# A decayed linear attention with a Fourier mix and an MLP: five instruction queues written anew

## The chip, the cores and the metric

The kernel runs on one core of one Trainium2 chip. The metric is the device time of one execution in microseconds (us). A core has five engines with a queue each: TensorE (PE, matmuls), ScalarE (ACT), VectorE (DVE), GpSimd (POOL) and SyncE (SP, which here only issues transfers). A queue is worked off in its written order, and an instruction that waits for a semaphore holds up all that stand behind it on the same engine.

## The reference

There are 4 batches, 8 heads, 768 positions and a head width of 48, so 384 model columns. The reference, cut to what matters:

```python
for t in range(S):                                   # per batch and head
    y[t]  = r[t] @ (state + outer(u * k[t], v[t]))
    state = w[t][:, None] * state + outer(k[t], v[t])
x = y.transpose(0, 2, 1, 3).reshape(B, S, 384)
u = x + real(fft(fft(x, axis=1), axis=2))            # Fourier mix
un = (u - mean(u)) / sqrt(var(u) + 1e-6)
out = u + maximum(un @ w_ch1, 0) @ w_ch2             # 384 -> 1536 -> 384
```

## The kernel before

**Work.** A batch is cut into 6 chunks of 128 positions. For each chunk the *attention* part takes the logarithm of w (line 754), sums it by a matmul with a triangular mask (756, 760, 766/769), takes exponentials (762, 775), multiplies r and k by them (794, 797), transposes both (810 and 816 on TensorE, for the last batch 802 by a transfer), forms the 128 x 128 products of all heads (826), masks them (839), updates the state (860, 868) and sums the output (881/884, added to v times the bonus in 890). Batch 0 does this for two chunks at a time, with its own lines (607 to 736; the product of k and decay is line 659, its transposes 666, the masks 688, the state 704/708, the outputs 722 to 730). The bonus is r times k (642 or 779), times u (643 or 781), a sum over the head (644 or 783) and the product with v (647 or 786). Line 789 casts v.

The *mix* part of a batch folds the attention's output by symmetry (901 to 922), multiplies by cosine and sine tables (948), copies and mirrors the result (953, 957), multiplies again (971), adds x (973), takes mean and variance (977, 979), writes the normalized rows (983), transposes them (994/997, or for batches 2 and 3 a transfer, line 1000), and then for each half of a batch runs the MLP: 12 x 3 matmuls of 384 columns (1018), the ReLU (1025 on ScalarE, 1023 on VectorE), 3 x 12 matmuls (1036), the last sum (1040) and the output (1044). Batches overlap: the mix of batch b runs beside the attention of batch b+1.

**Order.** Each operation is made once, in program order, with a number, its reads and its writes; from these `place` and `emit` derive the semaphores. The order on each queue does not follow from the program: `ORDER` holds, for each of the five queues, the list of operation numbers in the order of issue, and so also says which engine does an operation that may run on several (`vec`: POOL or VectorE; `evict`: ScalarE or VectorE). `BANKS` holds, for each of the 8 PSUM banks, the order in which tiles use it; a tile waits for the former tile of its bank.

```python
def place(self, order, banks):
    self.order = {e: [self.ops[int(i)] for i in order[e].split()] for e in self.ENGS}
    for e in self.ENGS:
        for o in self.order[e]:
            o.eng = e
            o.fn = o.alts[e][1]
```

**Loads.** All loads of w, k, r and v are issued by SyncE (494 for batch 0, 384 KB each; 500 for the others, 192 KB each), into 7 buffers per tensor, so a load also waits until its buffer's former content has been read. The two weight matrices (1152 KB each, line 587) are issued by POOL. The outputs (1044) and the transposing transfers (802, 1000) stand in SyncE's queue among the loads.

**Filler matmuls.** Eight matmuls at the start (1056) and `NW` more (1073), which read a constant tile and whose results nobody reads, are placed by `ORDER` like any other.

**Numbers used below.** On the start (batch 0): 43, 93, 140 are the loads of w for chunks 0/1, 2/3, 4/5; 48, 95, 142 those of k; 47, 94, 141 those of r. 50, 97, 144 are the logarithms; 54, 57 the exponentials of the first pair of chunks, 101, 104 those of the second. 66, 68 are the products of k and decay of chunks 0 and 1; 113, 115 of chunks 2 and 3 (the second pair, "chunk 2" in the lists). 60, 61, 62 are the first pair's bonus steps. In batch 1, 368 is the load of k of chunk 0 and 376 its product with r. In batch 3, 1175 is r times k of chunk 4; 1124 the product of k and decay of chunk 2.

Of the kernel before, what the change touches and what calls it, by code (L numbers as in the profile page):

```python
# [22 lines left out]
NW = 12  # L23
# [10 lines left out]

W_AFTER = {"W1": (0, 4, "w"), "W2": (1, 0, "r")}
# [26 lines left out]
    "act": (  # L62
# [12 lines left out]
    "dve": (  # L75
# [14 lines left out]
    "pool": (  # L90
# [12 lines left out]
}  # L103

BANKS = (
# [220 lines left out]
def bass_rwkv6_finch__then__fnet_fourier_mix_kernel(  # L326
# [19 lines left out]
    NJ = HID // 128  # L346
# [760 lines left out]
```

## Time and profile before

| | |
|---|---|
| median of 3 runs | 189.91 us (186.45 to 191.11) |
| the profiled execution's own time | 187.31 us |
| its span, first to last instruction | 185.5 us |
| mean granted TensorE clock | 0.991 |
| TensorE, VectorE, ScalarE, POOL busy | 95%, 84%, 64%, 54% |
| instructions on these | 1827 matmuls, 346, 280, 115 |
| bytes moved by transfers | 29.59 MB, mean 160 GB/s |
| instruction packets (two queues) | 0.23 MB and 0.06 MB |

A row of the table by stages gives the stretch in us, its length, then busy time and number of instructions for PE, weight loads, VectorE, ScalarE and POOL, the granted clock, the share of the 16 transfer engines and GB/s. Rows of groups give line, engine, operation, what is written and read, shapes, the count, busy us in all, mean ns of one, and the idle time before them with what ended it. Rows of the chain of work that ended last give start, length, and what it was. Rows of waits give us in all, times, and the longest. The mean length that stands for a matmul is that from its start to its modelled end; those of 384 columns have 326 ns there, and where nothing stops them 21 of them take 3.41 us.

### The profile page before, as it was taken

The numbers are of one execution on the slowest core, as the hardware profiler recorded it, in microseconds if no ns is written. First come the engines' busy times: TensorE is split into PE (matmuls) and PEld (weight loads), VectorE is DVE, ScalarE is ACT, GpSimd is POOL, SyncE is SP. The second block draws the span as 40 slices with busy tenths as digits, with TensorE's granted clock in tenths as the row PEclk, the third lists the DMA queues.
The fourth block names the chain that finished last, engine by engine and source line by source line (L and its number), as shares of the span: only waits on it lengthen the run. The fifth ranks groups of instructions, "written<-read, shape, count | busy, mean of one in ns | idle before, by whom it ended". The sixth has DMA issues, their size and how long they took to land.

```text
span 185.5 us, 4700 instructions
## 1 busy us (share of the span) xinstructions
PE 176.3 (95%) x1827; PEld 115.0 (62%) x1827; DVE 155.8 (84%) x346; ACT 119.3 (64%) x280; POOL 100.0 (54%) x115
## 2 busy tenths in 40 slices
PE   6986999998997999999999999998999999999994
PEld 2463776865565677666767765564676656565663
DVE  7599898799999989999999999998997938627034
ACT  3696699599989959789999585993452334222200
POOL 4186687599298744998997279959801000000000
PEclk9998799999999999999999999999999999999999
DMA  5999899899999999959677989988502131501233
GB/s 155 323 325 334 187 173 208 158 199 201 208 154 179 212 182 208 196 117 217 130 170 164 199 191 222 179 146 153 121 2 91 39 64 25 166 4 42 85 121 134
DMA packets 104151, 29.59 MB, mean 160 GB/s; under 512 B 98881, under 2 KB 103618, under 8 KB 104130
## 3 DMA queue, kind: packets, MB, share of 16 engines
q1 hardware_dynamic: 102178, 26.95, 65.3%
q0 software_dynamic: 1952, 2.36, 7.9%
q8 instruction: 14, 0.23, 0.4%
q14 instruction: 7, 0.06, 0.1%
HBM read 24.19 MB, written 4.72 MB: 156 GB/s over the span
## 4 chain that ended last, share of the span: by engine, by line
PE 70%; DVE 18%; DMA 6%; ACT 3%; issue 1%; SPq 0%; ACTq 0%
PE bank L1036 22%; PE bank L1018 19%; PE bank L971 5%; PE bank L948 5%; DVE ah L839 3%; DVE bst L977 2%; DMA unt<-un 2%; DMA in_v<-in_v_dram 2%; PE bank L826 2%; DMA in_w<-in_w_dram 2%; DVE uf L973 2%; PE bank L726 1%; PE bank L722 1%; DVE rkh L794 1%; PE bank L760 1%
## 5 line engine op out<-in xcount | busy, mean ns | idle before, releaser
L1018 PE MATMUL bank<-unt,w 128*128 128x384 bf16 x288 | 55.5, 326 | 0.6 <-DMA unt<-un 0.5
L1036 PE MATMUL bank<-w,ht 128*128 128x384 bf16 (+2 forms) x300 | 53.3, 320 | 0.0
L1025 ACT ACTIVATE ht<-bank 128x384 bf16<-128x384 f32 x74 | 34.4, 496 | 28.3 <-PE bank L1018 28.1
L1036 PEld LDWEIGHTS bank<-w,ht 128*128 128x128 bf16 x300 | 27.8, 98 | 15.9
L1018 PEld LDWEIGHTS bank<-unt,w 128*128 128x128 bf16 x288 | 26.3, 97 | 16.2 <-DMA unt<-un 0.9
L451 POOL TENSOR_TENSOR rkh<-in_k,e 128x384 bf16<-128x384 f32 x20 | 20.6, 1028 | 9.9 <-ACT e L634 8.4
L1040 DVE SCALAR_TENSOR_TENSOR osb<-bank,rstd,uf 128x384 f32<-128x384 f32 (+2 forms) x25 | 14.8, 595 | 12.0 <-PE bank L1036 11.9
L839 DVE TENSOR_TENSOR ah<-bank,msk 128x512 bf16<-128x512 f32 x36 | 23.4, 676 | 0.4 <-PE bank L826 0.3
L474 ACT ACTIVATE rkt<-bank 128x512 bf16<-128x512 bf16 (+1 forms) x26 | 18.0, 712 | 5.0 <-PE bank L810 2.8
L451 POOL TENSOR_TENSOR rk<-rk,ub 128x384 f32<-128x384 f32 x17 | 16.9, 998 | 4.4 <-DVE rk L451 4.1
L451 POOL TENSOR_TENSOR rk<-in_r,in_k 128x384 f32<-128x384 f32 x16 | 16.2, 1022 | 2.9 <-DMA in_k<-in_k_dram 2.8
L451 POOL TENSOR_TENSOR vtd<-in_v,dc 128x384 f32<-128x384 f32 x17 | 14.3, 842 | 4.1 <-DVE dc L783 4.1
L1023 DVE TENSOR_SCALAR ht<-bank 128x384 bf16<-128x384 f32 x22 | 11.6, 547 | 5.5 <-PE bank L1036 5.1
L465 ACT ACTIVATE lb<-in_w 128x384 bf16<-128x384 f32 (+1 forms) x21 | 11.9, 571 | 2.5 <-DMA in_w<-in_w_dram 2.5
L973 DVE TENSOR_TENSOR uf<-bank,x 128x384 f32<-128x384 f32 x24 | 12.5, 545 | 0.6 <-PE bank L971 0.6
L977 DVE BATCH_NORM_STATS2 bst<-uf 128x6 f32<-128x384 f32 x24 | 12.9, 546 | 0.0
L948 PE MATMUL bank<-k,xf 128*128 128x193 bf16 (+1 forms) x84 | 11.6, 258 | 0.0
L890 DVE TENSOR_TENSOR x<-bank,vtd 128x384 f32<-128x384 f32 x18 | 9.9, 548 | 1.8 <-POOL vtd L451 1.1
L465 ACT ACTIVATE un<-uf,agg 128x384 bf16<-128x384 f32 x17 | 10.4, 627 | 0.1
L465 ACT ACTIVATE vb<-in_v 128x384 bf16<-128x384 f32 (+1 forms) x17 | 9.4, 558 | 1.6 <-DMA in_v<-in_v_dram 1.6
L794 DVE TENSOR_TENSOR rkh<-bank,in_r 128x384 bf16<-128x384 f32 x18 | 9.7, 546 | 0.4 <-ACT bank L762 0.4
L762 ACT ACTIVATE bank<-bank 128x384 f32<-128x384 f32 x18 | 8.7, 487 | 2.0 <-PE bank L756 2.0
(144 smaller groups left out, 355.9 us busy)
## 6 DMA issues: line engine op xcount, KB each, us to landing
out_dram<-osb SPq DMA_DIRECT2D x23, 192.0 KB, 2.0
in_w<-in_w_dram SPq DMA_DIRECT2D x18, 192.0 KB, 4.5
in_v<-in_v_dram SPq DMA_DIRECT2D x18, 192.0 KB, 4.0
in_r<-in_r_dram SPq DMA_DIRECT2D x18, 192.0 KB, 4.4
in_k<-in_k_dram SPq DMA_DIRECT2D x18, 192.0 KB, 4.3
w<-in_moe_w_ch_dram POOLq DMA_DIRECT2D x2, 1152.0 KB, 10.8
in_w<-in_w_dram SPq DMA_DIRECT2D x3, 384.0 KB, 4.7
in_k<-in_k_dram SPq DMA_DIRECT2D x3, 384.0 KB, 4.6
```

Source lines behind the costliest of these rows:

```text
L451: return lambda e: e.tensor_tensor(out=o, in0=a, in1=b, op=f)
L465: return lambda e: e.activation(o, a, f, **kw)
L474: {"act": lambda e: e.activation(o(), i(), ACTF.Copy), "dve": lambda e: e.tensor_copy(out=o(), in_=i())}, **kw)
L839: masked[n] = op("dve", v_1(512), lambda e, x=x: e.tensor_tensor(out=ah[:, x:H:2, :], in0=ps(ta[x])[:, :].rearrange("p (h t) -> p h t", t= ...
L948: return e.matmul(ps(t)[:, cols], x, tab[:, s % NP, cols], start=a, stop=z, skip_group_check=True)
L973: op("dve", v_1(DM), lambda e, kb=kb, t=t: e.tensor_tensor(out=uf[:, kb, :], in0=ps(t)[:, 0:DM], in1=xb[:, kb, 0:DM], op=ALU.add), r=[t, ( ...
L977: op("dve", v_1(DM), lambda e, kb=kb, bs=bs: e.bn_stats(bs[:, :], uf[:, kb, :]), r=[("UF", i, kb)], w=[("BST", n % 4)])
L1018: ins = e.matmul(ps(t)[:, 0:384], W1[:, m, 128 * j:128 * j + 128], unt[:, :, m, :], start=(m == 0), stop=(m == NM - 1))
L1023: {"dve": lambda e, j=j, t=t, ht=ht: e.tensor_scalar(out=ht[:, j, :], in0=ps(t)[:, 0:384], scalar1=-1.0, scalar2=0.0, op0=ALU.mult, op1=AL ...
L1025: "act": lambda e, j=j, t=t, ht=ht: e.activation(ht[:, j, :], ps(t)[:, 0:384], ACTF.Relu, scale=-1.0)},
L1036: ins = e.matmul(ps(t)[:, 0:hi - lo], ht[:, j, 128 * x:128 * x + 128], W2[:, j, lo:hi], start=(j == 0), stop=(j == NJ - 1))
L1040: op("dve", v_1(hi - lo) + 64, lambda e, kb=kb, t=t, o=o, lo=lo, hi=hi: e.scalar_tensor_tensor(out=o[:, lo:hi], in0=ps(t)[:, 0:hi - lo], s ...
```

## The change

`NW` goes from 12 to 20, and `ORDER` and `BANKS` are new in full. `W2C = 0` is a new switch; with 0 the weight's load and its use are what they were.

```diff
-NW = 12
+NW = 20
+W2C = 0
...
     "pe": (
-        "24 1383 1384 52 53 51 55 56 1385 98 99 45 70 100 69 71 72 81 1386 102 1387 103 87 1388 75 78 149 146 117 "
-        "147 116 119 145 1389 118 128 89 122 83 192 195 125 1390 163 162 1391 165 164 372 134 401 374 189 403 130 "
+        "1383 1384 24 1385 55 52 53 51 99 56 98 1386 45 102 70 100 72 103 81 69 71 146 87 1387 147 1388 117 1389 "
+        "1390 1391 75 78 119 145 116 118 128 1392 1393 1394 122 125 89 83 1395 149 1396 195 192 401 1397 403 372 "
+        "1398 189 374 162 164 1399 1400 163 1401 165 130 134 168 171 136 208 200 209 201 174 371 400 176 180 202 "
...
     "act": (
-        "0 50 54 97 58 59 57 46 101 105 73 74 144 104 106 111 148 121 152 120 151 150 90 193 196 370 399 84 166 "
+        "0 50 97 54 58 57 59 46 105 101 144 106 73 104 74 111 121 120 148 151 399 152 90 84 187 150 370 193 186 "
...
     "dve": (
-        "36 30 10 1 7 5 35 33 11 29 12 17 21 39 26 4 13 37 16 15 27 18 22 31 9 6 8 19 20 23 66 188 60 65 67 64 61 "
-        "82 62 107 88 112 80 115 114 76 77 79 109 160 129 124 158 123 194 127 126 154 155 135 169 170 173 172 175 "
+        "11 33 5 1 7 9 6 13 12 10 39 28 36 17 38 15 16 35 32 34 14 21 18 8 23 20 19 22 66 60 68 64 65 4 67 82 62 "
+        "107 112 88 114 77 79 76 188 80 123 126 109 129 160 127 158 124 194 190 154 155 135 170 173 169 172 175 "
...
     "pool": (
-        "2 42 38 3 41 34 25 68 113 32 28 63 108 153 159 161 110 91 86 85 132 156 92 139 138 178 376 198 207 405 "
+        "29 31 30 26 2 25 3 27 61 113 115 63 108 153 159 110 161 86 91 92 85 156 132 139 405 198 207 229 411 469 "
...
+        "835 834 882 865 1098 1092 1093 1066 1067 1175 1124 1176 1095 1069 1118 1150 1144 1119 1181 1145 1121 "
...
     "sp": (
-        "43 48 93 47 44 49 95 94 140 96 142 141 185 395 366 143 424 453 398 487 369 367 368 455 396 397 425 426 "
+        "43 93 48 47 44 49 140 95 94 96 142 141 395 185 366 143 424 367 396 454 453 369 398 397 368 426 455 487 "
...
-            asked[n] = op("pool", d, lambda e, T=T, x=x: e.dma_start(T[:, :, :], x.rearrange("(q p) n -> p q n", p=128)),
+            asked[n] = op("pool", d, lambda e, T=T, x=x, n=n: e.dma_start(
+                T[:, :, :], x.rearrange("(p q) n -> p q n" if n == "W2" and W2C else "(q p) n -> p q n", p=128)),
...
-                        ins = e.matmul(ps(t)[:, 0:384], W1[:, m, 128 * j:128 * j + 128], unt[:, :, m, :],
+                        ins = e.matmul(ps(t)[:, 0:384], W1[:, m, j::NJ] if W2C else W1[:, m, 128 * j:128 * j + 128], unt[:, :, m, :],
```

78 operations are on another engine than before. By kind of work (the line that makes them), the number that goes each way:

| line, work | |
|---|---|
| 578, 581 fills | 6 VectorE to POOL, 4 POOL to VectorE |
| 643 bonus times u, batch 0 | 1 VectorE to POOL (op 61) |
| 659 k times decay, batch 0 | 115 VectorE to POOL, 68 POOL to VectorE |
| 779 r times k | 2 VectorE to POOL, 1 POOL to VectorE (op 376) |
| 786 bonus times v | 1 VectorE to POOL (batch 1, chunk 3) |
| 789 cast of v | 3 VectorE to ScalarE |
| 797 k times decay | 1 POOL to VectorE |
| 819, 820 copies of transposed r, k | 6 ScalarE to VectorE, 3 VectorE to ScalarE |
| 901 fold, batch 0 | 2 POOL to VectorE |
| 915 to 920 folds | 8 VectorE to POOL, 2 POOL to VectorE |
| 953 copies in the mix | 4 VectorE to ScalarE |
| 957 mirrors in the mix | 2 POOL to ScalarE, 1 ScalarE to POOL |
| 983 normalized rows | 6 VectorE to ScalarE |
| 997 copies of transposed rows | 1 ScalarE to VectorE |
| 1022 ReLU | 11 ScalarE to VectorE, 9 VectorE to ScalarE |
| 549, 567 tables | 1 VectorE to ScalarE, 1 ScalarE to VectorE |

After it VectorE has 331 instructions instead of 346, ScalarE 288 instead of 280, POOL's list 118 instead of 111, TensorE's list 545 instead of 537; SyncE's 121 are the same in another order.

134 rows, old and new, of tables (BANKS, ORDER) are left out of this document.

## The prediction

> **What bounds the kernel now.** I read the page first, then the busy time by stages, then the chain that ended last, then the waits.
>
> ```profile
> span 185.5 us, 4700 instructions
> PE 176.3 (95%) x1827; PEld 115.0 (62%) x1827; DVE 155.8 (84%) x346; ACT 119.3 (64%) x280; POOL 100.0 (54%) x115
> ...
> PE 70%; DVE 18%; DMA 6%; ACT 3%; issue 1%; SPq 0%; ACTq 0%
> ```
>
> TensorE carries the chain for 70% of the span and VectorE for 18%, but not at the same time. So the stages:
>
> ```profile
> core 0: us, PE busy (x) PEld busy (x) DVE busy (x) ACT busy (x) POOL busy (x), PEclk, DMA share, GB/s
> 0.00:13.70 13.70, 11.50 (x129) 6.45 (x129) 10.52 (x42) 8.77 (x14) 6.08 (x16) 1.00 0.97 267
> 13.70:17.10 3.40, 1.74 (x25) 1.30 (x25) 3.40 (x5) 1.83 (x4) 2.67 (x2) 1.00 1.12 360
> 17.10:20.50 3.40, 3.36 (x32) 1.98 (x30) 3.27 (x6) 2.81 (x4) 2.68 (x2) 0.50 0.78 165
> 20.50:38.00 17.50, 17.50 (x303) 13.05 (x301) 15.00 (x29) 13.27 (x31) 12.28 (x16) 1.00 0.97 191
> 38.00:59.10 21.10, 19.02 (x218) 12.36 (x216) 21.03 (x47) 19.69 (x47) 17.54 (x19) 1.00 1.05 189
> 59.10:129.00 69.90, 69.20 (x755) 46.25 (x752) 67.27 (x145) 56.63 (x140) 53.56 (x59) 1.00 0.90 179
> 129.00:185.50 56.50, 53.98 (x380) 33.64 (x378) 35.30 (x78) 16.28 (x43) 5.15 (x6) 1.00 0.26 76
> ```
>
> Four stretches can be seen. Until 20.5 us loads and a stall bind. TensorE is busy for 1.74 of 3.40 us, and in the next 3.4 us its granted clock is 0.50. From 38.0 to 59.1 VectorE is never idle (21.03 of 21.10) and TensorE has 2.1 us of holes. From 59.1 to 129.0 both are full. After 129.0 TensorE alone is full up to the last output.
>
> ```profile
> 0.73 3.42 DMA in_w<-in_w_dram
> ...
> 6.23 0.50 ACT e L634
> ...
> 14.72 2.08 DVE rkh L451
> 16.84 0.42 PE bank L666 x4
> ...
> 55.32 0.47 DVE bank L868
> ...
> 124.53 3.84 DMA unt<-un
> 128.41 1.64 PE bank L1018 x9
> ...
> 155.65 3.41 PE bank L1018 x21
> ...
> 171.90 11.09 PE bank L1036 x80
> 183.02 0.35 DVE osb L1040
> ```
>
> The chain begins with a load, then hangs on one VectorE product of 2.08 us (k times the decay, line 659, chunk 2 of batch 0) for which the transposes of line 666 wait. It runs through VectorE up to 55.8 us, and at the end through matmuls 0.16 us apart (3.41 us for 21). So the span is the matmul work plus what TensorE loses before 59.1 us and a little at 124.5. A gain has to come from these; the stretch after 129.0 can only grow.
>
> **The change part by part.** The operations are the same but for eight more filler matmuls. W2C = 0 leaves the weight lines as they are, and the end is unchanged: last product, last output. All five queues, the engine of 78 operations and the PSUM banks are new. I follow the new lists with the durations of the old rows:
>
> ```profile
> L451 POOL TENSOR_TENSOR rkh<-in_k,e 128x384 bf16<-128x384 f32 x20 | 20.6, 1028 | 9.9 <-ACT e L634 8.4 <-ACT e L775 0.8 <-DMA in_k<-in_k_dram 0.6
> L451 DVE TENSOR_TENSOR rkh<-in_k,e 128x384 bf16<-128x384 f32 x4 | 3.7, 931 | 1.6 <-ACT e L634 1.6
> L451 DVE TENSOR_TENSOR vtd<-in_v,dc 128x384 f32<-128x384 f32 x1 | 1.3, 1349 | 0.0
> L791 DVE CAST vb<-in_v 128x384 bf16<-128x384 f32 x3 | 2.4, 790 | 0.0
> L475 DVE COPY rkt<-bank 128x512 bf16<-128x512 bf16 x4 | 1.7, 413 | 0.0
> L890 DVE TENSOR_TENSOR x<-bank,vtd 128x384 f32<-128x384 f32 x18 | 9.9, 548 | 1.8 <-POOL vtd L451 1.1 <-PE bank L884 0.5
> L475 DVE COPY unt<-bank 128x384 bf16<-128x384 bf16 x1 | 0.3, 340 | 0.0
> L1073 PE MATMUL bank<-ht 128*128 128x384 bf16 x12 | 4.3, 380 | 0.0
> ```
>
> *Term 1, up to 38.0 us.* The 2.08 us product (op 115) goes to POOL, where it takes 1.03 (first row), and in exchange op 68 of chunk 0 comes to VectorE (0.93). The second product of the bonus (op 61) goes to POOL too. On POOL the order is then 61, 113, 115, and op 115 waits for its exponential (op 104), which ScalarE reaches earlier because the third w load (op 140) is now issued ahead of op 95. I put the end of op 115 at 14.2 us instead of 16.8: its exponential, which starts at 13.43 in the rows below and ends at 13.9, ends 0.8 earlier without the logarithm of w (0.84) just ahead of it, and then 1.03 for the product. Against this stands the order of the loads. Each of these 384 KB pieces takes 1.2 us at the rate of this stretch:
>
> ```profile
> GB/s 155 323 325 334 187 173 208 158 199 201 208 154 179 212 182 208 196 117 217 130 170 164 199 191 222 179 146 153 121 2 91 39 64 25 166 4 42 85 121 134
> 12.67 0.84 ACT L465 ACTIVATE lb<-in_w 128x768 bf16<-128x768 f32 x1 [0.20 <-DMA in_w<-in_w_dram]
> 13.43 0.48 ACT L634 ACTIVATE e<-bank 128x392 f32<-128x392 f32 x1
> L500 SPq DMA_DIRECT2D in_k<-in_k_dram x18: 436/784/4297, 25.6 to 119.4; - x18
> L462 POOL MEMSET rkh<- 128x128 bf16 x3 | 0.6, 205 | 0.0
> ```
>
> (325 GB/s, slices two to four.) The k and r of chunk 2 are one piece later, so VectorE's three products on them move 1.2 us back. The masks and the second half of the first pair come out about 2 us earlier. The stall of 13.7 to 17.1 shrinks, and with it the half clock that follows, if no other stall takes its place. In batch 1, k of chunk 0 (op 368) is issued two places later, 1.6 us at the median of 784 ns an issue. It then lands about when VectorE's op 376, which is new there, wants it, and up to 1.6 us is given back. Bounds: -2.7 us (2.6 of the product, and a bit of clock) and +0.5 (loads decide, and the masks start up to 0.8 later behind four POOL fills of 205 ns, which VectorE's own fills cover now). I take -1.3, a little beyond the middle, since the row nearest to it is the product. ScalarE's first exponential stands now behind the logarithm of chunk 2, which waits for the second load; that one lands some 1.2 us after the first, at 5.4, and the logarithm is done at 6.2, when the exponential starts anyway (6.23).
>
> *Term 2, 38.0 to 59.1 us.* Here each VectorE operation taken away is worth its time until TensorE's holes are filled. Up to the masks of chunk 3 of batch 1, VectorE loses one product v times bonus (1.35), two casts of v (2 x 0.79), two copies of transposes (2 x 0.41) and two sums x (2 x 0.55, done later), 4.9 us. It gains four copies of transposes (4 x 0.41) and one of unt (0.34), 2.0 us. That is -2.9 by the rows. TensorE's holes are 2.1, so this is what can be had without TensorE doing more. ScalarE takes the casts and gives copies, and stays under VectorE's load there (19.69 of 21.10); POOL's fills and products before that point balance. Bounds 0 and -2.9; I take -1.9, since the gain ends where the holes end.
>
> *Term 3, after 59.1 us.* Up to the last attention output VectorE has 5.6 us less to do in all (the 15 fewer instructions, 331 after 346, are folds, products, casts and copies). TensorE's visible idle time there is 0.7 us up to 129.0, and the unt transfer at 124.5 holds the chain for 3.84, of which the matmuls waited little:
>
> ```profile
> PE bank L826 <- DVE rkt L475: 1.2, 1, 1.2
> ...
> PE bank L1018 <- DMA unt<-un: 0.5, 1, 0.5
> ```
>
> Bounds 0 and -2.0 (0.7, and small gaps that the modelled ends hide); I take -0.8.
>
> *Term 4, the fillers.* Eight matmuls at one issue interval (3.41/21 = 0.16) are 1.3 us. Three old ones and seven new stand now between the first transposes of batch 0 and its third pair, where TensorE waits. Hidden there they cost nothing; behind a queue that has just been freed, all 1.3. I take +0.4.
>
> *ScalarE and POOL.* ScalarE has 8 more operations, about 4.4 us at 0.5 to 0.6 each, POOL 7 more, 6.9 us. ScalarE's cover is its own waiting, POOL's is 85 us of idle time, of which 16 lie between 59.1 and 129.0.
>
> ```profile
> ACT ht L1025 <- PE bank L1018: 28.1, 18, 5.1
> ...
> POOL rkh L451 <- ACT e L634: 8.4, 3, 6.1
> ```
>
> *Banks and outputs.* Each PSUM tile waits for the former one of its bank, and the pairs are new. No wait of TensorE on a bank's release is among its longest, so I cost it at nothing; without that cover it is one wait of the size above, 1.2 us. Outputs stand now at other places among the loads of SyncE, and what they delay is the ring below.
>
> **The sum** is made against the profiled execution, 187.31 us with a span of 185.5, so 1.8 lie around the span. 185.5 - 1.3 - 1.9 - 0.8 + 0.4 = 181.9, and with 1.8 it is 183.7. The runs shown have a median of 189.91 (186.45 to 191.11), 2.6 above the profiled execution. That scatter is wide, and what causes it is not in the trace; a plan with less standing just in time should keep part of it. I add half, 1.3: **185.0 us**.
>
> **The clock.** The Trainium skill ("TensorE: Matmul & The Clock Gate", section "What's actually happening") says that a window of about 3.4 us without enough matmul work puts the array on half clock, and that the windows run freely. The trace agrees: 1.74 of 3.40 busy, then 3.4 us at 0.50. [...]
>
> **The rivals.**
> - *The start stays with the loads (B).* For it: DMA share 0.97 to 1.12 until 17.1 us, and two chunk-2 loads and the k of batch 1 issued later. Against it: the chain hung on a product, not on a load, at 14.7 us. Then term 1 is 0, the half clock stays, and the fillers are paid in full: 185.5 - 1.9 - 0.8 + 1.3 = 184.1, with 1.8 and 1.3 it is 187.2.
> - *More than forecast (C).* Term 1 whole (-2.7), term 2 up to the holes (-2.1), term 3 whole (-2.0), fillers free: 178.7, so 181.8. For it: TensorE would be full from 25 us on. Against it: every stage must give everything.
> - *A ring of POOL and SyncE (D), the slower side.* In batch 3 the new POOL list puts r times k of chunk 4 (op 1175) ahead of k times decay of chunk 2 (op 1124). The r and k that it needs are issued behind the transposing transfer of chunk 0, and those of chunk 5 behind that of chunk 3, which needs POOL again. Behind op 1124 all later POOL work of batch 3 is queued, and TensorE waits for that through the transposes. A load lands in 4.2 us, but it can be 11.0:
>
> ```profile
> DMA to landing us min/median/max: 2.9/4.2/11.0
> 110.00:129.00 19.00, 18.30 (x187) 11.22 (x184) 17.50 (x40) 13.91 (x34) 16.13 (x19) 1.00 0.93 176
> ```
>
>   Two such loads cost 2 x 6.8 = 13.6 less POOL's 2.9 of idle time there, +10.7 on 185.0, so 195.7 at the worst. It passes the old median from +4.9 on, when both land after some 8.1 us. Middle: 192.8. Against it: the long landings lie at 34 to 63 us, beside the weights, not in batch 3.
> - That the change doesn't do what it says can't be excluded for the loads: if the instruction packets fall elsewhere, their order is no better. That time is B's.
>
> **How the numbers follow.** Forecast 0.52 (own range 183.0 to 187.0), B 0.27, C 0.13, D 0.08. The range goes from 181.5 (just past C) to 189.5, which leaves D and a little of each end outside. A measurement of this kernel can tell about 2% from no change, which is 186.1 and 193.7 here. Faster: three quarters of the forecast, all of C and a little of B, 0.55. Slower: most of D, 0.07. Within 2%: 0.38.
>
> **What would show it.** Right: the product of line 659, chunk 2, on POOL ending before 15 us; granted clock 1.00 from 17.1 to 20.5; the first matmul of line 971 near 36.5 instead of 38.0; VectorE with idle time between 38 and 59; TensorE's holes after 45 us under 1 us; VectorE idle by 3 us and more between 59 and 129. Term 2 is wrong if VectorE is still full there and the masks of chunk 3 end after 58 us. Wrong altogether: a half-clock stretch in a new place, or POOL waiting for in_r or in_k of batch 3 by more than 3 us, with TensorE idle after 110 us.

## The result and the profile after

| | before | after |
|---|---|---|
| median of 4 runs each | 188.52 us (186.45 to 191.11) | 184.25 us (183.24 to 185.52) |
| profiled execution, its span, its granted clock | 187.31, 185.5, 0.991 | 183.24, 181.4, 1.000 |
| ratio of the undisturbed runs, 95% interval | | 0.9891 [0.9853, 0.9929] |

A second measurement (run e5 below) gave 184.52 us and 0.9891 [0.9833, 0.9949]. The ratio says 1.1%, the medians 2.3%, because the ratio leaves out the runs in which the granted clock stayed at half for several stretches; of 65 runs of the kernel before that were taken beside the experiments 37 were such (mean clock 0.973 or less, 189.2 us and more). A stretch of 3.4 us at half clock takes 1.7/185 = 0.009 off a run's mean clock, so 0.991 stands for one such stretch and 0.973 for three. By the ratio the change stays within 2% of before, the outcome that the prediction gave 0.38, against 0.55 for more than 2% faster. Among runs at a mean clock of 0.998 and more, the kernel before took 185.98 us (mean of 10, 185.4 to 186.7), the changed one 184.00 (mean of 7, 183.2 to 184.8): 2.0 us less. I call these "full-clock means" below.

The first rows of the page and the chain by engine, after:

```profile
span 181.4 us, 4708 instructions
PE 175.2 (97%) x1835; PEld 114.7 (63%) x1835; DVE 146.9 (81%) x331; ACT 123.8 (68%) x288; POOL 107.9 (59%) x122
...
PE 87%; SPq 4%; DVE 3%; DMA 3%; ACT 1%; issue 0%; DVEq 0%
```

VectorE's share of the chain fell from 18% to 3%. The busy time by the same stages as before, after:

```profile
13.70:17.10 3.40, 3.13 (x58) 1.98 (x58) 3.40 (x8) 2.87 (x4) 3.40 (x3) 1.00 1.05 261
17.10:20.50 3.40, 2.54 (x67) 1.73 (x65) 3.40 (x6) 2.24 (x6) 3.40 (x3) 1.00 1.01 269
20.50:38.00 17.50, 17.48 (x262) 12.55 (x259) 15.52 (x32) 14.27 (x33) 12.01 (x15) 1.00 0.97 185
38.00:59.10 21.10, 20.89 (x247) 13.62 (x246) 20.79 (x50) 20.80 (x52) 20.14 (x24) 1.00 1.08 189
59.10:129.00 69.90, 69.87 (x766) 47.02 (x764) 65.64 (x140) 58.97 (x147) 59.86 (x64) 1.00 0.98 193
```

Two stages moved: TensorE is busy 3.13 instead of 1.74 between 13.7 and 17.1, with a full clock behind it, and 20.89 instead of 19.02 between 38.0 and 59.1. VectorE's load there is hardly lower (20.79 after 21.03), it is still full; but its masks of chunk 3 of batch 1 end at 55.2 us instead of 58.4. From 59.1 to 129.0 it has 4.3 us of idle time. The start, in the chain after:

```profile
7.96 4.94 DMA in_r<-in_r_dram
12.99 0.96 DVE uf L453
...
15.35 1.79 DVE ht L691 x3
17.14 1.00 DVE unt L457
...
18.89 0.48 PE bank L725 x2
```

A load of r now carries it to 12.9 us, and at 17.14 stands an operation of 1.00 us that I had not thought of: the scaling that makes the negative identity (op 188). Line numbers differ by up to 3 between the kernels.

### The profile page after: what moved, and what is told of

Its sections match the earlier page's. It is cut to its first block, busy times and chain, and to the rows that moved or that the text cites. A ratio compares the mean times of both kernels' runs of the same rounds, so it can differ in the third digit from the quotient of the medians.

```text
span 181.4 us, 4708 instructions
## 1 busy us (share of the span) xinstructions
PE 175.2 (97%) x1835; PEld 114.7 (63%) x1835; DVE 146.9 (81%) x331; ACT 123.8 (68%) x288; POOL 107.9 (59%) x122
## 4 chain that ended last, share of the span: by engine, by line
PE 87%; SPq 4%; DVE 3%; DMA 3%; ACT 1%; issue 0%; DVEq 0%
PE bank L1021 26%; PE bank L1039 26%; PE bank L974 6%; PE bank L951 5%; SPq L496 3%; PE bank L829 3%; DMA in_r<-in_r_dram 3%; PE bank L887 2%; PE bank L759 2%; PE bank L763 2%; PE bank L813 1%; PE bank L819 1%; PE bank L884 1%; PE bank L863 1%; PE bank L725 1%; DVE ht L691 1%
## 5 line engine op out<-in xcount | busy, mean ns | idle before, releaser
L1021 PE MATMUL bank<-unt,w 128*128 128x384 bf16 x288 | 55.2, 326 | 0.0
L1028 ACT ACTIVATE ht<-bank 128x384 bf16<-128x384 f32 x72 | 33.9, 518 | 23.8 <-PE bank L1021 18.4
L453 POOL TENSOR_TENSOR rkh<-in_k,e 128x384 bf16<-128x384 f32 x19 | 19.7, 1038 | 5.3 <-ACT e L778 4.6
L1026 DVE TENSOR_SCALAR ht<-bank 128x384 bf16<-128x384 f32 x24 | 12.3, 547 | 10.4 <-PE bank L1021 10.4
L453 POOL TENSOR_TENSOR rk<-in_r,in_k 128x384 f32<-128x384 f32 x17 | 17.1, 1012 | 3.3 <-DMA in_k<-in_k_dram 1.9
L476 ACT ACTIVATE rkt<-bank 128x512 bf16<-128x512 bf16 (+1 forms) x23 | 16.7, 729 | 3.5 <-PE bank L813 2.8
L453 POOL TENSOR_TENSOR vtd<-in_v,dc 128x384 f32<-128x384 f32 x18 | 15.2, 848 | 0.4 <-DVE dc L786 0.3
L467 ACT ACTIVATE un<-uf,agg 128x384 bf16<-128x384 f32 x23 | 13.9, 621 | 1.7 <-DVE agg L982 1.7
L453 POOL TENSOR_TENSOR xf<-sd 128x382 bf16<-128x382 f32 (+1 forms) x11 | 11.5, 1058 | 3.0 <-DMA in_k<-in_k_dram 1.6
L951 PE MATMUL bank<-k,xf 128*128 128x193 bf16 (+1 forms) x84 | 12.7, 258 | 0.0
L467 ACT ACTIVATE vb<-in_v 128x384 bf16<-128x384 f32 (+1 forms) x20 | 11.4, 570 | 0.2 <-DMA in_v<-in_v_dram 0.2
```

The costliest lines, as they stand in the source:

```text
L453: return lambda e: e.tensor_tensor(out=o, in0=a, in1=b, op=f)
L467: return lambda e: e.activation(o, a, f, **kw)
L476: {"act": lambda e: e.activation(o(), i(), ACTF.Copy), "dve": lambda e: e.tensor_copy(out=o(), in_=i())}, **kw)
L951: return e.matmul(ps(t)[:, cols], x, tab[:, s % NP, cols], start=a, stop=z, skip_group_check=True)
L1021: ins = e.matmul(ps(t)[:, 0:384], W1[:, m, j::NJ] if W2C else W1[:, m, 128 * j:128 * j + 128], unt[:, :, m, :], start=(m == 0), stop=(m == ...
L1026: {"dve": lambda e, j=j, t=t, ht=ht: e.tensor_scalar(out=ht[:, j, :], in0=ps(t)[:, 0:384], scalar1=-1.0, scalar2=0.0, op0=ALU.mult, op1=AL ...
```

## The experiments

Three theories went in. **V**: VectorE's shorter list between 38 and 59 us gives the gain, the start adds little. **S**: the start gives it, through the products that changed engine. **O**: only the plan as a whole is worth something. From the second round on two more: **F**, the new fillers hold the granted clock, against **V+**, the plan is shorter at any clock.

| run | median us | ratio to before, 95% | full-clock mean (runs) | runs at 0.985 or less |
|---|---|---|---|---|
| before | 189.5 | | 185.98 (10) | 37 of 65 |
| e1 start only | 189.76 | 1.0146 [1.0089, 1.0204] | none | 5 of 6 |
| e2 rest only | 190.11 | 1.0173 [1.0116, 1.0229] | none | 6 of 6 |
| e3 engines only | 188.21 | 0.9967 [0.9928, 1.0007] | 185.55 (5) | 6 of 12 |
| e4 no new fillers | 188.20 | none | 182.91 (1) | 4 of 6 |
| e5 changed again | 184.52 | 0.9891 [0.9833, 0.9949] | 184.17 (5) | 1 of 6 |
| e6 fillers only | 187.07 | 1.0021 [0.9977, 1.0066] | 186.38 (8) | 0 of 12 |
| e7 op 188 early | 184.43 | 0.9855 [0.9795, 0.9915] | 183.79 (4) | 2 of 6 |
| e8 new to 59 us | 185.77 | 0.9942 [0.9905, 0.9980] | 185.26 (7) | 3 of 12 |
| e9 start swap | 188.47 | 1.0115 [1.0070, 1.0161] | none | 4 of 6 |
| e10 engines, fillers | 187.10 | 1.0025 [0.9983, 1.0066] | 186.69 (9) | 2 of 12 |
| e11 engines undone | 186.62 | 0.9968 [0.9918, 1.0019] | 185.21 (4) | 3 of 12 |
| e12 op 188 first | 184.16 | 0.9876 [0.9831, 0.9921] | 183.72 (3) | 1 of 6 |

### Halves of the plan: e1, e2 and e8

Here S20 (S59) is the set of operations that one plan starts before 20 us (59.1 us), closed so that nothing in it waits for something outside. The seam is the same on all queues and banks.

```diff
-ORDER[e] = OLD[e]
+ORDER[e] = [i for i in NEW[e] if i in S20] + [i for i in OLD[e] if i not in S20]   # e1, 17 fillers
+ORDER[e] = [i for i in OLD[e] if i in S20] + [i for i in NEW[e] if i not in S20]   # e2, 14 fillers
+ORDER[e] = [i for i in NEW[e] if i in S59] + [i for i in OLD[e] if i not in S59]   # e8, 20 fillers
```

> The new plan up to about 20 us (143 operations with the nine fillers among them), the old plan for everything else. Nothing is left out. Theory V (most of the gain comes from VectorE's shorter list between 38 and 59 us, the start adds little): 0.3 to 1.0 us less than the kernel before, since the first half of the second pair came 1.0 us earlier but the y of chunk 3 not at all. Theory S (the start gives it, and what TensorE wins there is kept to the end): 2.5 us less or more. Theory O (only the plan as a whole is worth something, a seam costs): no gain, or up to 1 us more.

> The old plan up to about 20 us, the new plan for the rest: the counterpart of the first run. V: 3.0 to 3.6 us less than before (2.9 in 38 to 59, 0.3 later). S: 1 us less at most. O: within 1 us of before. If the two runs together give the whole (4 us), the parts add up; if they give less, start and rest need one another.

> The new plan up to 59.1 us (495 operations), the old one for everything later. V: at equal clock 2.0 us or more less than the kernel before, so nearly all of the 2.3; after 59 us the two plans are worth the same. O (a plan is worth something only as a whole): at least 1 us of it is lost at the seam, as in the runs with a seam at 20 us.

Both seams at 20 us lost: no run of either at full clock, and 1.5 and 1.7% more than before. (Of e1's 17 fillers 14 come from the new start; the nine of its expectation are a slip.) For e2 that loss is the clock: its three runs at a mean clock of 0.971 to 0.973 took 188.3 to 190.1 us, and the kernel before 189.9 at that clock (mean of 36). e1 is slower at equal clock too: its one run at 0.991 took 188.6 us, against 186.7. So these times do not say whether start and rest add up. The third stage says more, first with the new start and the old rest (e1), then with the old start and the new rest (e2):

```profile
38.00:59.10 21.10, 19.07 (x216) 12.83 (x213) 20.75 (x46) 19.10 (x45) 16.15 (x18) 1.00 1.00 181
```

```profile
38.00:59.10 21.10, 20.89 (x230) 13.95 (x228) 19.66 (x49) 19.87 (x48) 17.26 (x19) 1.00 1.03 189
```

In these profiles what TensorE gains there goes with the new rest, and the old start ahead of it takes nothing away. The stages of e1 at its seam:

```profile
17.10:20.50 3.40, 2.54 (x74) 1.98 (x73) 3.40 (x6) 2.00 (x5) 3.39 (x5) 1.00 0.99 283
20.50:23.90 3.40, 1.83 (x10) 0.57 (x8) 2.78 (x6) 0.98 (x2) 0.82 (x3) 0.64 0.86 185
23.90:27.30 3.40, 3.40 (x26) 2.59 (x25) 2.78 (x3) 1.90 (x4) 3.40 (x4) 0.50 1.02 202
```

Right behind the seam TensorE finds 10 matmuls in 3.4 us, and the clock is halved within that stretch (0.64) and behind it (0.50). Probably the new start leaves other work over than the old one, and the old list behind it has none to offer; that is not tested. e8, with the seam at 59.1, is 0.7 us better than before at full clock (185.98 - 185.26) where V had asked for 2.0, and 1.1 better than e6, which has as many fillers:

```profile
38.00:59.10 21.10, 20.89 (x248) 13.55 (x245) 20.77 (x49) 20.79 (x51) 20.13 (x24) 1.00 1.08 188
59.10:129.00 69.90, 68.24 (x740) 45.49 (x740) 66.95 (x144) 55.47 (x138) 52.50 (x57) 1.00 0.94 183
```

It has the whole gain of the third stage (20.89) and loses 1.6 us of it behind the seam (68.24 after 69.87), where the old list in its own place has 69.20. That is O's loss at the seam. With e1 and e2 it puts TensorE's gain between 38 and 59 us; but of the time, less than half of the gain was left at the end of e8.

### The engines of ten operations: e3, e10 and e11

```diff
-act 386 414 443 267 472   dve 385 438 467 507 466
+act 385 438 467 507   dve 386 414 443 267 472   pool 466      # e3: in the old lists; e10: with e6's fillers too
-act 385 438 467 507   dve 386 414 443 267 472   pool 466
+act 386 414 443 267 472   dve 385 438 467 507 466             # e11: in the new lists
```

> The old plan with nothing changed but the engine of ten operations between 38 and 59 us, each at the place in the other engine's list that belongs to its old time: the product v times bonus of chunk 3 to POOL, two casts of v and two copies of transposes to ScalarE, four copies of transposes and one of unt to VectorE. VectorE's ledger there changes by -1.35 -0.79 -0.79 -0.41 -0.41 +4x0.41 +0.34 = -1.8 us (the two sums x stay). V: 1.2 to 1.8 us less than before, with idle time on VectorE between 38 and 59. O (the order must fit the engines): no gain, or a loss up to 1 us, since the four copies that VectorE gains stand in a full list.

> The old plan with the same eight fillers, and the engines of the ten operations between 38 and 59 us changed as in the run engines only. To be read against fillers only at full clock. V (VectorE's ledger there, -1.8 us): 1.2 to 1.8 us less, and TensorE's holes between 40 and 60 us fall from 5.3 to about 3.5. O (the order must fit the engines): 0.5 us less at most (engines only gave 0.3 at full clock), holes over 4.5.

> The changed kernel with the engines of the same ten operations put back to the old ones, each at the place that belongs to its time in the new plan. To be read against the changed kernel at full clock (183.2 to 184.8, mean 184.0). V: 1.2 to 1.8 us more, VectorE without idle time from 38 to 57 us. O: under 0.6 us more, the order of the lists being what gives the gain.

On the old order the engines alone are worth nothing that can be measured (0.4 us at full clock in e3; e10 has 0.3 more than e6). The stage of e10 shows what came of them:

```profile
38.00:59.10 21.10, 19.68 (x222) 12.47 (x222) 19.76 (x49) 19.56 (x47) 17.44 (x19) 1.00 1.07 196
```

VectorE did get its 1.3 us of idle time (19.76 after 21.03), near the ledger's 1.8. TensorE got only half of it, 0.66, and the runs kept none. V's rule "each VectorE operation taken away is worth its time" falls here. In the new order, undoing the same ten costs 1.2 us (185.21, four runs from 184.3 to 186.4, after 184.00, seven runs from 183.2 to 184.8):

```profile
38.00:59.10 21.10, 19.93 (x220) 12.13 (x219) 20.39 (x45) 21.03 (x50) 18.11 (x22) 1.00 1.09 194
```

Against e6, which has as many fillers, the engines alone are 0.3 us worse (e10), the new order without them 1.2 better (e11), and both together 2.4 better. So both seem to be needed: the engines in an order that uses them (O, with V's size). Full proof it is not: the runs are few, and the changed kernel's second profile (e5) has 19.84 in this stage, like e11; its first, e2, e4, e7, e8 and e12 have 20.85 to 20.89.

```profile
38.00:59.10 21.10, 19.84 (x231) 12.66 (x229) 19.77 (x47) 19.94 (x49) 18.99 (x23) 1.00 1.08 186
```

### The fillers and the clock: e4, e5 and e6

```diff
-NW = 20      "pe": ... 83 1395 149 1396 195 192 401 1397 403 ... 260 1402 261 ...
+NW = 12      "pe": ... 83 149 195 192 401 403 ... 260 261 ...                       # e4, from the changed kernel
-NW = 12      "pe": ... 87 1388 75 ... 145 1389 118 ... 125 1390 163 ...
+NW = 20      "pe": ... 87 1388 1389 1390 1391 1392 75 ... 145 1393 1394 1395 1396 118 ... 125 1397 1398 163 ...   # e6, from before
```

> The new plan without its last eight fillers (those between 20 and 24.5 us and the one at 40), so 12 as before. Nothing of the computation is left out. If they are paid in full, 0.16 us each: 1.3 us less than the changed kernel, some 5.4 us less than before. If they lie in waiting time as I costed them (0.4 paid): 0.4 less than the changed kernel. If their work keeps the granted clock up: a half-clock stretch shows between 17 and 31 us and the time is up to 1.7 us more than the changed kernel.

> The changed kernel itself once more, beside the others, since the kernel before ran from 185.6 to 196.7 us with its granted clock between 1.000 and 0.939, and at a clock of 1.000 its three runs lie at 185.6 to 186.1. Theory V+ (the plan is shorter at any clock): 183.2 to 183.9 at 1.000, so 2.3 us less than before at the same clock, and the rest of the difference of the medians is the clock, with which the plan has little to do: then runs at 0.97 and less are as frequent as with the kernel before (9 of 17). Theory F (the new fillers hold the clock): no run under 0.99.

> The old plan with nothing but eight more fillers, where the new plan has most of its own: four at 12.5 us, three at 17.9, one at 23.3. F: the share of runs under 0.99 falls from 9 of 17 to 2 of 6 or less, and the median falls by 2 us or more (to 186.5 to 187.5). V+: clock as before, and 0.4 to 1.3 us more at the same clock, since the four at 12.5 stand ahead of the intra-chunk products.

At the same clock the fillers seem to cost about what I had costed: 186.38 - 185.98 = 0.4 us in the old plan, which is hardly clear of the scatter (eight runs from 185.6 to 187.4, ten from 185.4 to 186.7); e4's one full-clock run is 182.91, 1.1 under the changed kernel's mean. But they hold the clock. Eight fillers alone took the old plan from 37 of 65 runs with several half-clock stretches to 0 of 12; without its eight, the new plan fell into them in 4 of 6. Both F and V+ are right, about different things, though F's "no run under 0.99" missed by one of e5's six (0.981). The old plan with them (e6), and without them in an execution with such stretches (e3, whose start is the old one):

```profile
13.70:17.10 3.40, 2.02 (x45) 1.31 (x33) 3.40 (x5) 2.10 (x5) 2.70 (x2) 1.00 1.07 307
17.10:20.50 3.40, 3.23 (x53) 2.02 (x53) 3.32 (x7) 2.81 (x4) 2.36 (x2) 1.00 0.84 202
...
38.00:59.10 21.10, 19.02 (x218) 12.33 (x216) 21.03 (x47) 19.69 (x47) 17.12 (x18) 1.00 1.07 191
59.10:129.00 69.90, 69.81 (x768) 47.01 (x767) 68.00 (x147) 56.92 (x141) 54.38 (x58) 1.00 0.92 181
```

```profile
13.70:17.10 3.40, 1.69 (x25) 1.28 (x25) 3.40 (x5) 1.85 (x4) 2.73 (x2) 1.00 1.13 362
17.10:20.50 3.40, 3.33 (x33) 1.92 (x31) 3.33 (x6) 2.81 (x4) 2.77 (x2) 0.58 0.87 189
20.50:23.90 3.40, 3.40 (x53) 2.31 (x50) 2.31 (x4) 0.87 (x2) 1.36 (x2) 0.50 1.14 238
23.90:27.30 3.40, 3.40 (x38) 2.59 (x37) 2.75 (x4) 1.86 (x5) 2.93 (x4) 0.50 0.82 161
```

1.69 busy of 3.40 was followed by about 10 us at half clock, 2.02 by none. The busy time of one stretch does not decide it alone: from 17.1 to 20.5 e11 had 2.53 and then a clock of 0.52, the changed kernel 2.54 and then 1.00. e6 is also the fair partner for the new plan, with as many fillers and the same clock: 186.38 against 184.00 us, so 2.4; 19.02 against 20.89 in the stage from 38.0, and no difference behind it (69.81 against 69.87).

### The start's products: e9, e7 and e12

```diff
-pool 68   dve 61 115
+pool 61 115   dve 68                                # e9: in the old lists, with e6's fillers
-"dve": ... 22 66 60 ... 79 76 188 80 ...
+"dve": ... 22 66 188 60 ... 79 76 80 ...            # e7: in the new lists
+"dve": ... 22 188 66 60 ... 79 76 80 ...            # e12
```

> The old plan with the eight fillers of the run before (fillers only) and three products at the start changed between the engines as in the new plan: k times decay of chunk 2 (op 115) and the second bonus product (op 61) to POOL, k times decay of chunk 0 (op 68) to VectorE. To be read against fillers only, at full granted clock (185.6 to 187.4 there). Theory S (the start's products shorten the chain, my term 1): 1.0 to 2.0 us less. Theory P (what the start wins is gone by the y of chunk 3 of batch 0, since that came at 28.07 with the old start and 28.27 with the new at full clock): within 0.5 us, with op 115 ending 1 to 2 us earlier all the same.

> The changed kernel with one operation moved on VectorE: the scaling that makes the negative identity (op 188; 1.08 us at 17.06 in the changed kernel's profile, ahead of the masked product that the second pair waits for) stands right after the first product of chunk 0, where VectorE waits for r anyway. Theory N (what the start had won was lost again to this operation): the second pair's first half ends 0.6 to 1.0 us earlier, and up to 0.8 us of it is left at the end. Theory L (the loads of chunk 3 and the next batch set what comes later): the second pair earlier, but the end within 0.3 us of the changed kernel.

> The changed kernel with the scaling that makes the negative identity (op 188) ahead of VectorE's first product of chunk 0, where VectorE waits for the exponential for over 2 us. At its former place (run e7) it ran in 0.25 us, but what followed came 0.2 later, and the cast of v then began 0.09 after a POOL product of 1.85 us and took 2.17 in place of 0.55. Theory N+ (a VectorE operation of this kind waits for the POOL product that is under way, and that alone cost it): op 188 takes 0.25, the cast 0.55, y of the second pair's first half comes 0.8 to 1.0 earlier than in the changed kernel; the end 0 to 0.8 us earlier. L: the end within 0.3 of it.

e9 missed both expectations: op 115 came later, not earlier, and the ratio is 1.0115. It is no fair test of S. Its edit put op 115 on POOL behind ops 63 and 108 (61, 113, 63, 108, 115), and in the changed kernel it stands ahead of both (61, 113, 115, 63); so in e9 it began only at 18.19 us. Its rows, then those of e7:

```profile
10.02 1.81 POOL L450 TENSOR_TENSOR uf<-uf,ub 128x768 f32<-128x768 f32 x1 [7.35 <-ACT ub L473]
...
18.19 0.99 POOL L450 TENSOR_TENSOR rkh<-in_k,e 128x384 bf16<-128x384 f32 x1
...
10.21 2.04 DVE L652 CAST vb<-in_v 128x768 bf16<-128x768 f32 x1
```

```profile
7.52 0.25 DVE L454 TENSOR_SCALAR unt<-idw 128x384 bf16<-128x384 bf16 x1
...
9.33 2.17 DVE L652 CAST vb<-in_v 128x768 bf16<-128x768 f32 x1
...
9.24 1.85 POOL L450 TENSOR_TENSOR uf<-uf,ub 128x768 f32<-128x768 f32 x1 [6.58 <-ACT ub L473]
```

The cast takes 0.55 us when it starts ahead of POOL's product, and over 2 when it starts 0.09 or 0.19 behind it: it ends 0.4 after POOL. In e9 TensorE then waited 1.3 us for it (the state, line 708), and half clock followed. e7 moved op 188 to an idle place, where it took 0.25, but everything behind came 0.2 later, and the cast lost that race. e12, with op 188 earlier still, won it:

```profile
4.39 0.25 DVE L454 TENSOR_SCALAR unt<-idw 128x384 bf16<-128x384 bf16 x1
...
9.17 0.55 DVE L652 CAST vb<-in_v 128x768 bf16<-128x768 f32 x1
```

Here is what that did to the outputs of batch 0 (the first two products of each chunk; the last two numbers are the start of the first and of the last in us): the kernel before, e6, the changed kernel's two profiles, e12.

```profile
L722 PE MATMUL bank<-vtd,ht x12: 322/332/524, 19.4 to 31.9; 64*128 64x384 bf16 x12
```

```profile
L722 PE MATMUL bank<-vtd,ht x12: 322/328/333, 19.3 to 31.4; 64*128 64x384 bf16 x12
```

```profile
L725 PE MATMUL bank<-vtd,ht x12: 320/323/333, 18.9 to 31.4; 64*128 64x384 bf16 x12
```

```profile
L725 PE MATMUL bank<-vtd,ht x12: 320/323/333, 18.6 to 31.2; 64*128 64x384 bf16 x12
```

```profile
L722 PE MATMUL bank<-vtd,ht x12: 322/328/333, 17.7 to 30.2; 64*128 64x384 bf16 x12
```

The last of them starts at 31.4 in the old plan with fillers and at 31.2 to 31.4 in the new: at equal clock the new start wins at most 0.2. With op 188 out of the way it is 1.0 to 1.2 earlier (N+ right). The end did not follow clearly: 183.72 at full clock after 184.00, and the ratios' intervals overlap. Its profile has a new half-clock stretch from about 32 us, which can have cost what was won. Whether e12 beats the changed kernel stays open; if so, by some 0.3 us.

## Why the prediction was right, point by point

The forecast was 185.0, the medians are 184.25 and 184.52, and the profiled execution was forecast at 183.7 and took 183.24. The sum came out partly by luck. The execution that met 183.7 is the fastest of ten; at full clock the mean of seven is 184.00, so like for like (below) 2.7 us were gained where the sum had 3.6. Of the terms, the first was too large and had the wrong cause, and the third came to next to nothing.

- **Term 1, the start: size and cause wrong.** -1.3 was to come from op 115 going to POOL. That product did end earlier (14.82 instead of 16.79, not 14.2), and the gain was gone by the last output. What the start gave is the clock: 31.9 to 31.4 with fillers alone, and 186.73 to 185.98 between runs at 0.99 (mean of 18) and at full clock, so 0.5 to 0.75 us (on the medians it is more, 2.4 us in e6). The step that failed is "the 2.08 us product": it was one of some 0.55 us that waited for POOL. Before, and after:

```profile
14.56 1.80 POOL L451 TENSOR_TENSOR uf<-uf,ub 128x768 f32<-128x768 f32 x1
...
14.72 2.07 DVE L451 TENSOR_TENSOR rkh<-in_k,e 128x384 bf16<-128x384 f32 x1
```

```profile
13.10 1.72 POOL L453 TENSOR_TENSOR rkh<-in_k,e 128x384 bf16<-128x384 f32 x1 [0.37 <-ACT e L637]
14.77 1.47 POOL L453 TENSOR_TENSOR vtd<-in_v,dcp 128x768 bf16<-128x768 f32 x1
16.21 1.82 POOL L453 TENSOR_TENSOR uf<-uf,ub 128x768 f32<-128x768 f32 x1
...
12.99 0.96 DVE L453 TENSOR_TENSOR uf<-in_r,in_k 128x768 f32<-128x768 f32 x1 [0.52 <-DMA in_r<-in_r_dram]
...
17.06 1.08 DVE L457 TENSOR_SCALAR unt<-idw 128x384 bf16<-128x384 bf16 x1
```

  On POOL it took 1.72, not the 1.03 of its row, since it now waited for VectorE (12.99 to 13.95), and the wait that was removed came back at op 188 (1.08 in place of 0.25). Of its group of four (3.7 us in all in the row that I quoted) the other three took (3.7 - 2.07)/3 = 0.54 each; that should have made me ask what this one stood beside.
- **Term 2, 38.0 to 59.1: place right, size right in one profile of two.** -1.9 was forecast, and TensorE's busy time rose by 1.87 (0.82 in e5). The reasoning, ledger of VectorE's operations up to the holes, gives only a bound: the engines without the order gave nothing (e10). And some of the ledger's prices were waits, as in term 1. The 1.35 us of v times bonus began beside a product of POOL; alone, in e11, the same operation took 0.54. Before, and e11:

```profile
53.97 1.35 DVE L451 TENSOR_TENSOR vtd<-in_v,dc 128x384 f32<-128x384 f32 x1
...
53.82 2.35 POOL L451 TENSOR_TENSOR rk<-in_r,in_k 128x384 f32<-128x384 f32 x2
```

```profile
56.37 0.54 DVE L450 TENSOR_TENSOR vtd<-in_v,dc 128x384 f32<-128x384 f32 x1
```

  One of the casts took 0.97 us behind a POOL product (47.01, that from 46.76 to 47.76); a cast of twice the size took 0.55 in e12.
- **Term 3, after 59.1: nearly nothing.** -0.8 was forecast. From 59.1 to 129.0 the new plan has 69.87, the old one 69.20 and, in e6, 69.81. VectorE's 4.3 us of idle time are there, but TensorE is already full.
- **Term 4, the fillers: +0.4 about right, the main effect missed.** I costed them as work to be hidden. They set how often the clock falls.
- **The step from profile to median, +1.3: right in size, cause not known then.** The scatter of the kernel before that I could not place is for the most part the granted clock (at full clock 1.3 us of it are left, 185.4 to 186.7). The changed kernel's median stays 1.0 to 1.3 above its profiled run because that was its fastest.
- **Rivals.** B has the start right (a load of r carries it to 12.9, and its products gain nothing) and the clock wrong. D did not come: over the whole execution POOL's products waited for in_k and in_r by 1.9 and 1.4 us at most, and of these only the 1.4 lies in batch 3.

```profile
POOL rk L453 <- DMA in_k<-in_k_dram: 1.9, 1, 1.9
...
POOL rk L453 <- DMA in_r<-in_r_dram: 1.4, 1, 1.4
```

- **The signs.** The product ended before 15 us, the clock was 1.00 from 17.1, VectorE had over 3 us of idle time after 59.1, and TensorE was busy for 14.10 of 14.10 us from 45.0 to 59.1. One failed in the main: VectorE was to have idle time between 38 and 59, and had 0.3 us (1.3 in e5). It stayed full, but the masks of chunk 3 came 3.2 us earlier, so of the two signs against term 2 only the first showed. The first matmul of line 971 was misread: it began at 36.89 before (38.0 is the first on the mirrored half) and at 36.16 after.

Like for like, from 186.73 (before at 0.99) to 184.00 are 2.7 us: 0.75 of clock, 1.9 of the stage from 38.0, less 0.4 of fillers; the 0.5 that are left I can't place (with e5's 0.8 for that stage, 1.6 are left).

## What to carry to other kernels

An instruction that is much longer in one place than its like elsewhere has waited inside its own row: look at what its neighbour engine ran at that moment before its time is counted as work that can be moved. Taking work off a full engine gave nothing here until the lists of the others were ordered to use it, so an edit that is tried alone can show nothing, and half of a plan can be worse than none. Before a scatter between runs is put down to chance, the granted clock of each run is to be read: eight fillers that cost some 0.4 us at full clock took 2.4 us off the median here (189.5 to 187.07).

## What the runs showed of the hardware

- **VectorE and POOL lock each other out, in some operations.** When a VectorE cast, scaling or product of two SBUF tiles meets a POOL product, whichever starts second ends after the first: the cast 0.55 to 2.04 and 2.17 us, the scaling 0.25 to 1.08, the product 0.55 to 2.07, POOL's product 1.00 to 1.72. VectorE's products with one input in PSUM (line 655, 0.55) run on beside POOL, and so do its sums over the head, though their input is in SBUF. Of the changed kernel:

```profile
45.95 1.01 POOL L453 TENSOR_TENSOR rk<-rk,ub 128x384 f32<-128x384 f32 x1
...
46.13 0.54 DVE L786 TENSOR_REDUCE dc<-rk 128x8 f32<-128x384 f32 x1
```

  The Trainium skill ("SBUF — State Buffer", section "Who interferes with whom") states this: the two share a pair of ports as an exclusive lock. The waits above agree; by that rule the 2.08 us of term 1 could have been read as 0.55 and a wait.
- **The clock answers to activity, and not the same way each time.** Stretches of 3.4 us with 1.56 (e2), 1.69 (e3) and 1.74 us of matmuls were followed by half clock, those with 1.92 (e10) and 2.02 (e6) were not; but 2.53 was in e11, and 2.54 in the changed kernel was not. So no threshold comes out of these traces. Once halved, the clock stayed so for 3.4 us in the kernel before and for about 10 us in e3, with TensorE busy nearly all the while. By its mean clock the same program ran at full clock in 10 of 65 runs, with one half-clock stretch in 18 and with several in 37.
- **At full clock one program still scatters** by 1.5 us (183.2 to 184.8); the two profiles of the changed kernel differ most between 38 and 59 us (20.89 and 19.84). What does that was not found.
